# A delta-rule attention and a multiplicative FFN in one kernel: two more weight buffers, outputs without a drain, and a new order of steps

## The chip, the cores and the metric

The kernel runs on one core of a Trainium2 chip. The metric is the device time of one execution in microseconds (us). Names of the engines: PE is the TensorE matmul engine (PEld its weight loads), DVE is VectorE, ACT is ScalarE, POOL is GpSimd, and SP is SyncE, which here only issues transfers.

## The reference

The first part is a delta-rule attention over 4 batches, 8 heads, 768 tokens and a head width of 48; the second an FFN over the 3072 tokens, in which two products are multiplied before the third. The four weights arrive as float64, all other inputs as float32; the kernel computes in float32.

```python
k_n = k / (np.linalg.norm(k, axis=-1, keepdims=True) + 1e-06)
for t in range(S):
    y[:, :, t] = q[:, :, t] @ state                    # per batch and head, 48 x 48 state
    v_old = state . k_n[t]
    state = state + beta[t] * outer(k_n[t], v[t] - v_old)
x = y.transpose(0, 2, 1, 3).reshape(B * S, H * D)      # 3072 x 384
a, b = x @ w1, x @ w2                                  # 3072 x 1024 each
out = ((a * b) @ w3) @ w_out                           # 3072 x 384
```

## The kernel before

**Chunks.** The 768 tokens are cut into 12 chunks of 64. In a chunk the recurrence becomes matrix products: `scores` (steps `s0` to `s11`) multiplies keys by keys and by queries; `to_blocks` (`u`) and `inverse` (`V0` to `V5`, one for two chunks) solve the triangular systems on DVE by 31 steps of multiply and subtract in blocks of 32; `corner` (`e`) joins the blocks by products on PE; `chain` (`c`) carries the state on, by three groups of products on PE with a step of DVE behind each; `outputs` (`y`) forms the chunk's outputs, by features, in the tile `xT`. Norms are made by `squares` (`g`) and `norms` (`N`), values are scaled by `scaled_v` (`n`). `load_k`, `load_q`, `load_v`, `load_perm` (`k`, `q`, `v`, `p`) issue transfers; `by_tensor` (`K`, `Q`) transposes the first two chunks on PE, `by_vector` (`d`) the others on DVE.

**Weights.** The 36 weight pieces (`P0` to `P35`) arrive as float64 and are turned into float32 by `piece`: a transfer by SP into a `raw` buffer (line 789), two ACT instructions (797, 798), two of DVE (800, 801) and an addition on POOL (805), behind which the buffer is free. `raw` has five buffers, taken in turn, so SP holds the sixth piece until POOL has finished with the first. `P0` to `P7` are `w_out`, `P8` to `P23` are `w3`, `P24` to `P35` are `w1` and `w2`. Then `w3` is transposed (`t`) and multiplied into `w_out` (`fold`, steps `f0` to `f7`, two halves of four products each; line 849), so that the FFN has one product less. The first half of a fold needs the first four pieces of `w_out`, the second half the last four. Five raw buffers later become room for sums of weights (`T`, `W`).

**FFN.** Two chunks make a unit of 512 tokens. Steps `a`, `b`, `h`, `i`, `j` form the products with `w1` and `w2` (lines 869, 988), `S` and `G` sums of blocks on POOL, `o` the last products (1098), `x` the results and their stores.

**Order.** No scheduler orders the instructions. `ORDER` is a list of some 1,460 names written out; each name runs its generator up to the next `yield`, and every engine, and every queue, works off its instructions in the order of that text. So an instruction that waits holds all that is behind it on its engine. Pools are turned by hand: `in_turn` gives out the next buffer of a tag. The PSUM tag `w` has two pairs of banks, and one is held while an inverse keeps its matrix there; the SBUF tag `o` has two buffers (squares, results), `xT` has two (beta, the inverses' columns, then the outputs).

**Scores and outputs.** Heads go in pairs, an even one on partitions 0 to 47, an odd one on 64 to 111, and batches in two halves `z`, so that four tiles of 64 rows by 64 columns of the array can be at work together. In `scores` an even head gets one matmul of 128 columns (lines 381 to 384: keys and queries at once), an odd head two of 64 (387), with the second written to the other half of the partitions. One copy on ACT (405) takes the query part, `PT`, out of PSUM, and POOL masks it (407). Chunks 2 and 3 do that on DVE (411). In `outputs` (line 744) a chunk's 64 matmuls are of two kinds, state by query and `X` by `PT`; those that would write a bank from other rows of the array than the rest come last, behind a drain of PE:

```python
        for mode, todo in enumerate(modes):
            if mode:
                drain = pe.drain().ins
```

Eight copies of 48 x 256 on ACT (765) bring the outputs into `xT`. A float32 matmul appears as two records in the trace.

Of the kernel before, what the change touches and what calls it, by code (L numbers as in the profile page):

```python
# [39 lines left out]
V0 P0 k0 beta P18 P13 P0 P18 P0 P0 P11 g0 P13 K0 P18 K0 P11 P18 P10 P13 P13 q0 P3 P3 P11 g0 beta  # L40
beta K0 K0 K0 k1 K1 P10 P11 P12 P3 P12 g0 g0 Q0 P10 g0 g0 g0 g0 g0 P8 Q0 Q0 Q0 K1 K1 K1 Q0 K1 P3
N0 P9 k2 P8 P8 P10 s0 P8 N0 g1 s0 s0 s0 s0 s0 s0 u0 q1 P2 Q1 P9 p2 P2 P12 P12 P9 Q1 g1 Q1 Q1 P2
u0 g1 Q1 d2 d2 u0 P5 P1 t0 t0 t5 t5 P9 t2 t2 P4 P6 s1 s1 P5 P5 P2 s1 P1 s1 s1 s1 u1 g1 P1 u1 u1
t4 V0 V0 P5 V0 V0 P4 t10 P7 P4 t3 t3 V0 V0 P1 f1 P6 P6 t4 V0 P7 V0 V0 t10 t1 P14 P7 P4 V0 f0 V0
P6 P16 P16 V0 V0 P7 t1 s0 P19 P19 P19 P19 V0 f1 P17 k3 p2 v1 V0 V0 P14 P14 P14 V0 f2 P17 f2 f0 V0
f2 P15 v0 P20 f1 t11 f0 P17 P17 f5 V0 V0 P16 t11 P16 t8 P15 V1 V0 t8 f5 t9 V0 V0 t6 P15 V0 n0 n0
f5 V0 V0 V0 V0 t9 P20 P20 V0 t6 P22 P22 P22 f4 P23 P23 V0 f4 f4 P21 P21 P15 t7 t7 V0 s1 V0 V0 V0
V0 g1 d2 d2 P22 f3 f3 P24 P20 g1 g1 p3 g1 P26 p3 P30 e0 e0 e0 t12 t14 e1 e1 g1 f3 e0 e0 d3 d3 N1
s2 s2 s2 P23 P23 t12 e0 f6 e0 p4 s2 P24 e1 e1 t14 s2 e0 P24 s2 P25 c0 P26 f7 u2 P30 P24 c0 e1 e1
P21 P21 d3 d3 y0 y0 P26 P26 P31 t15 t13 s3 s3 s3 s3 s3 s3 t13 c0 n1 n1 P32 t15 u2 u2 u3 c0 P30 f7  # L50
e1 P25 P25 P31 P31 P27 c1 c1 u3 u3 f6 e1 c1 V1 V1 V1 y0 P31 f6 f7 P25 P27 V1 V1 V1 V1 P30 b1 c1
N1 b1 v2 P32 V1 V1 P27 V1 s1 y1 y1 b2 V1 d4 V1 V1 P28 P29 P32 b2 P27 V2 V1 V1 V1 y1 b3 V1 V1 P28
P28 b0 P32 c1 b2 b2 b3 b1 b1 b0 P29 P29 b0 P29 a03 a03 a02 V1 b0 V1 d4 V1 V1 a01 V1 P28 V1 V1 a02
V1 P35 a01 a00 a00 n2 n2 a04 a04 b7 P33 P33 a05 a05 P34 P34 a01 a07 b7 V1 b4 b5 V1 V1 V1 V1 k4
a01 a07 k5 b5 b3 g2 b4 V1 V1 P35 V1 V1 g2 c1 e2 e2 e2 e2 a06 a06 g2 e3 e3 e3 b3 g2 g2 a00 a02 a02
p4 v3 d4 d4 p5 a00 e2 P34 c2 c2 e2 P34 e2 b6 P35 P35 e2 c2 c2 e3 a03 g2 g2 P33 b6 y2 g2 P33 g2 d5
d5 p5 c2 c2 y2 a04 e3 s4 N2 e3 s4 a03 s4 b6 b6 s4 s4 s4 s4 T e3 T T d5 n3 d5 a04 e3 b4 b4 b7 s5
n3 k6 g3 u4 s5 s5 s5 s5 s5 s5 b5 b7 b5 a05 T c3 c3 a06 a05 a06 u5 V2 p6 g3 a07 a07 c3 c3 g3 S0 S0
S0 V2 g3 V2 V2 N2 oD0 y3 y3 V2 V2 W oA0 S0 S0 V2 V2 S0 S0 S0 c3 v5 n5 V2 V2 S0 S0 S0 S0 V2 v4 oB0
V2 V2 V2 xA0 V2 V2 xB0 V2 V2 oA0 S0 S0 S0 n4 oB0 xA0 d6 y3 k7 xA0 V2 n4 oC0 V2 V2 V2 a10 xB0 S0  # L60
V2 V2 xC0 G1 V2 xD0 a10 a10 V2 oC0 a10 a10 d6 xC0 xC0 xC0 xD0 V2 V2 i10 V2 h10 c3 c4 V2 V2 j10 V2
V2 V2 a10 h10 i10 a12 V2 V2 h10 W W a12 p6 V2 a12 a12 j12 e4 g3 g3 h10 c4 a12 h10 a12 h12 d6 d6
s5 i12 e4 e4 e4 i10 h12 h12 g3 g3 p7 g3 e4 e4 h12 N3 s4 h12 a11 a11 a11 s6 s6 i12 i12 e5 c4 j11
s6 c4 y4 y4 c4 e5 d7 d7 h11 c4 c5 a11 p7 e5 s6 a11 a11 h11 i11 i11 n5 c5 d7 d7 N3 a13 h11 h11 e5
W e5 s7 e5 a13 s7 s7 s7 s7 s7 s7 a13 a13 s6 s6 c5 i11 k8 u7 u6 g4 g4 g4 S1 V3 V3 c5 p8 h11 s6 g4
h13 a13 j13 a13 i13 h13 i13 i13 S1 h13 V3 h13 h13 V3 V3 y5 V3 V3 V3 V3 V3 V3 d8 V3 V3 V3 y5 oC1
oA1 S1 oD1 S1 S1 V3 V3 S1 xA1 c5 oA1 xA1 oB1 v6 y5 v7 a20 a20 V3 xA1 V3 V3 V3 d8 G2 V3 V3 xB1 n6
V3 V3 V3 V3 oB1 xB1 xC1 S1 j20 k9 V3 xD1 V3 V3 V3 V3 S1 oC1 a20 a20 p8 xC1 V3 xC1 h20 V3 xD1 xC1
V3 V3 V3 V3 a20 a20 i20 h20 a22 h20 g4 c5 g4 g4 g4 a22 V3 j22 d8 h20 h20 e6 i20 g4 a22 d8 a22 h22
a22 a22 i22 e6 V4 e6 c6 i20 h22 e6 i22 h22 n7 h22 e6 e6 a21 a21 a21 n6 c6 p9 c6 s8 i22 N4 h21 h22  # L70
i21 a21 s8 a21 s6 c6 y6 s8 s8 j21 s8 v8 a21 h21 i21 y6 d9 d9 e7 p9 e7 s8 s8 e7 e7 s7 h21 h21 i21
h21 a23 c6 c6 e7 a23 i23 a23 n8 n8 d9 e7 S2 N4 d9 a23 s9 s9 s9 s9 s9 n7 s9 k10 s9 u8 g5 a23 a23
c7 c7 h23 h23 i23 i23 c7 c7 g5 u9 h23 h23 V4 V4 V4 j23 h23 S2 g5 g5 V4 V4 V4 V4 p10 v9 V4 y7 y7
V4 V4 oA2 V4 V4 d10 V4 y7 V4 V4 S2 oD2 S2 d10 xA2 V4 S2 S2 oB2 oC2 V4 c7 xB2 V4 V4 V4 V4 oB2 xB2
xC2 xD2 p10 V4 V4 V4 oA2 V4 V4 a30 a30 G3 a30 a30 S2 S2 oC2 k11 V4 xC2 j30 s9 V4 xD2 xC2 V4 V4 V4
V4 V4 V4 xA2 xA2 xC2 g5 a30 h30 a30 i30 a32 h30 V4 V4 V4 e8 h30 i30 c7 a32 j32 h30 h30 g5 a32 a32
i32 g5 g5 d10 d10 i30 a32 a32 e8 h32 h32 i32 p11 e8 e8 a31 a31 c8 e8 s8 c8 g5 a31 j31 e8 c8 n9 c8
h32 h32 h32 y8 y8 c8 e9 e9 i31 d11 d11 h31 e9 e9 n9 a31 c8 s10 a31 p11 i32 N5 s10 s10 a31 h31 s10
s10 s10 s10 c9 c9 h31 e9 e9 d11 d11 u10 i31 i31 s11 a33 a33 S3 a33 v11 h31 h31 s11 s11 s11 s11
s11 a33 c9 i33 a33 a33 c9 h33 h33 s11 u11 i33 i33 j33 h33 h33 V5 V5 V5 V5 y9 S3 h33 V5 V5 V5 v10  # L80
n10 n10 oA3 S3 S3 V5 V5 oD3 V5 oB3 s10 y9 y9 oC3 V5 V5 S3 S3 V5 V5 V5 V5 V5 xA3 xB3 V5 V5 n11 V5
V5 oB3 V5 xB3 xD3 xC3 xC3 xD3 oA3 G4 a40 S3 S3 a40 a40 V5 oC3 N5 V5 V5 V5 xA3 a40 a40 xC3 h40 a40
h40 i40 V5 V5 V5 V5 h40 h40 V5 j40 h40 i40 V5 V5 V5 V5 a42 a42 a42 a42 i42 h42 a42 j42 xA3 V5 V5
a42 i40 h42 i42 h42 h42 a41 a41 a41 a41 h41 a41 V5 e10 e10 e10 e10 h42 n11 a41 i42 h41 i41 i41
i41 h41 e10 e11 h41 e10 c9 j41 a43 a43 a43 S4 c9 e11 e11 e11 h41 c10 c10 h43 c10 a43 e11 j43 xC3
a43 c10 a43 i43 h43 i43 i43 h43 h43 e11 h43 c10 c10 y10 y10 c11 s11 oD4 c11 c11 c11 oA4 xA4 y11
S4 S4 S4 oB4 oA4 y11 y11 S4 S4 S4 xA4 xB4 oB4 xB4 oC4 xC4 xA4 a50 xC4 S4 oC4 xC4 xD4 xD4 a50 G5
a50 h50 a50 a50 i50 a50 h50 i50 i50 h50 h50 j50 h50 a52 a52 a52 a52 i52 a52 a52 h52 a51 h52 i52
j52 h52 h52 h52 i51 a51 a51 a51 h51 i52 S5 a51 a51 h51 i51 j51 h51 h51 i51 a53 a53 a53 a53 h53
a53 a53 h53 j53 h51 h53 h53 h53 i53 i53 i53 xC4 o5 x5 o5 S5 S5 o5 o5 x5 S5 S5 S5 S5 o5 x5 x5 o5  # L90
x5 x5 x5 x5 x5 x5 S5 o5 x5 x5 x5 x5
# [4 lines left out]
def kernel(  # L96
# [14 lines left out]
    P = 128  # L111
# [21 lines left out]
    def half(z):  # L133
        return slice(C * z, C * z + C)
# [230 lines left out]
    def by_parity(x):  # L365
        return x.rearrange("p (a e) t -> p a e t", e=2)
# [3 lines left out]

    def scores(m):
        u = Us[m % 2][:, 0 : NR * H * C].rearrange("p (r h t) -> p r h t", r=NR, h=H)
        for r in range(NR):
            KQ = KQs[m]
            ps = two_banks()
            for h in range(H):
                for z in range(2):
                    x = KQ[feat(h % 2), NR * z + r, h // 2]
                    n = 128 * (h // 2)
                    if h % 2 == 0:  # L380
                        pe.matmul(  # L381
                            ps[half(z), 0, n : n + 128], lhsT=x[:, 0, :],
                            rhs=x.rearrange("p j t -> p (j t)"), start=True, stop=True,
                        )
                    else:
                        for j in range(2):
                            pe.matmul(  # L387
                                ps[half(z ^ j), 1, n + C * j : n + C * j + C],
                                lhsT=x[:, 0, :], rhs=x[:, j, :], start=True, stop=True,
                            )  # L390
# [13 lines left out]
            if m < 2 or m > 3:  # L404
                act.copy(out=by_parity(PT), in_=psv[:, :, :, 1, :])  # L405
                yield
                pool.tensor_tensor(  # L407
                    out=PT, in0=PT, in1=smask[:].unsqueeze(1).to_broadcast([P, H, C]), op=ALU.mult
                )
            else:  # L410
                dve.tensor_tensor(
                    out=by_parity(PT), in0=psv[:, :, :, 1, :],
                    in1=smask[:].unsqueeze(1).unsqueeze(1).to_broadcast([P, NP, 2, C]),
                    op=ALU.mult,
                )
# [295 lines left out]
    def outputs(c):  # L711
        PT, St, X, KQ = PTs[c], Ss.get(c), Xs[c], KQs[c]
        py = two_banks()
        pyv = py[:].rearrange("p x (b a t) -> p x b a t", b=B, a=2)

        def region(h, z, r):
            return pyv[feat(h // NP), (h + z) % 2, NR * z + r, h % NP // 2, :]
# [5 lines left out]
        for mode, todo in enumerate(modes):  # L723
# [8 lines left out]
            for r in range(NR if mode == 0 else 0):  # L732
# [5 lines left out]
        part = [(h // NP, (h + z) % 2) for todo in modes for h, z, *_ in todo]  # L738
        issued, n = ([], []), 0
        for mode, todo in enumerate(modes):  # L740
            if mode:
                drain = pe.drain().ins
# [7 lines left out]
        for i in issued[0]:  # L750
            in_order(i, drain)
# [7 lines left out]
        for z in range(2):  # L759
# [24 lines left out]

    def piece(n, srcs, dst):

        raw = in_turn(ffn, [P, CW, 2], "raw", 5, "raw", U32)
# [500 lines left out]
```

## Time and profile before

| What | Value |
|---|---|
| Median of 3 runs | 557.11 us (554.81 to 559.89) |
| Profiled execution, its own time | 556.14 us |
| Span of its trace | 554.1 us |
| PE busy | 520.0 us, 94% |
| DVE busy | 388.0 us, 70% |
| POOL busy | 256.6 us, 46% |
| ACT busy | 188.1 us, 34% |
| Chain that ended last | PE 74%, DVE 4%, ACT 1% of the span |
| Transferred | 52.64 MB, 95 GB/s on the mean |

The span is the time from the first to the last instruction in the trace; the execution's own time is 2.0 us more. Every duration below is from this one execution. A busy time is an engine's sum over the span, and says little on its own: a wait of DVE or ACT costs only if PE, in the end, waits for it.

### The profile page before, as it was taken

To read this page: it belongs to the slowest core of one execution; us is meant where nothing else is said; L and a number is where in the kernel's file an instruction comes from. 1 tells how busy PE (TensorE), PEld (TensorE's weight loads), DVE (VectorE), ACT (ScalarE), POOL (GpSimd) and SP (SyncE) were. 2 spreads that over 40 slices of the span, in tenths; PEclk is the share of its full clock that TensorE was granted. 3 is DMA by queue.
4 is the path that set the end of the run, shared out by engine and by line. 5 is a ranking of instruction groups with operands and counts; after the bars stand their busy time and mean duration, and the time that the engine had idled before them with its cause. 6 is when DMAs were issued, how large, how long until landed. Compare 5 with 4: busy or idle time off the path is not lost.

```text
span 554.1 us, 19883 instructions
## 1 busy us (share of the span) xinstructions
PE 520.0 (94%) x8540; PEld 446.7 (81%) x8540; DVE 388.0 (70%) x850; ACT 188.1 (34%) x393; POOL 256.6 (46%) x278
## 2 busy tenths in 40 slices
PE   2486998999999999999999999999999999999997
PEld 2473566688778988889988889988899888998897
DVE  3889999899876878659977579859587654123332
ACT  3688388954542112332022430123221121300000
POOL 8576473723659970455443355510482212342141
PEclk9998999999999999999999999999999999999999
DMA  8986987579457345455553564253411220020001
GB/s 247 197 200 211 161 224 126 138 157 151 63 80 128 76 110 82 60 100 89 99 108 64 82 120 76 92 83 46 106 31 44 63 50 2 10 66 1 0 1 57
DMA packets 197687, 52.64 MB, mean 95 GB/s; under 512 B 185344, under 2 KB 191488, under 8 KB 197600
## 3 DMA queue, kind: packets, MB, share of 16 engines
q1 hardware_dynamic: 193408, 50.59, 44.8%
q10 hardware_dynamic: 4192, 0.79, 1.0%
q8 instruction: 67, 1.10, 0.8%
q14 instruction: 20, 0.16, 0.1%
HBM read 41.25 MB, written 8.91 MB: 91 GB/s over the span
## 4 chain that ended last, share of the span: by engine, by line
PE 74%; DVE 4%; ACT 1%; issue 1%; DVEq 0%
PE ps_f L988 35%; PE ps_f L1098 19%; PE ps_w L645 5%; PE ps_w L744 4%; PE ps_f L869 4%; PE ps_w L574 2%; PE ps_w L381 1%; PE ps_w L387 1%; DVE ps_w L487 1%; DVE tb L482 1%; ACT TT L547 1%; PE ps_w L1098 1%; DVE KQ L337 0%; DVE ab L885 0%; DVE Ub L501 0%
## 5 line engine op out<-in xcount | busy, mean ns | idle before, releaser
L996 DVE TENSOR_TENSOR ab<-ab,ps_f 128x512 f32<-128x512 f32 x80 | 54.5, 682 | 58.5 <-PE ps_f L988 57.8
L1069 POOL TENSOR_TENSOR ab<-ab 128x512 f32<-128x512 f32 (+1 forms) x56 | 61.4, 1118 | 41.5 <-PE ps_f L1098 24.4
L988 PE MATMUL ps_f<-xT,w1s 128*128 128x256 f32 x320 | 78.5, 382 | 0.0
L1035 POOL TENSOR_TENSOR ab<-ab,late 128x512 f32<-128x512 f32 x19 | 24.2, 1272 | 107.6 <-DVE ab L996 106.1
L988 PEld LDWEIGHTS ps_f<-xT,w1s 128*128 128x128 f32 x320 | 59.9, 190 | 7.9
L1098 PE MATMUL ps_f<-w,ab 128*128 128x192 f32 x376 | 65.5, 328 | 0.0
L1098 PEld LDWEIGHTS ps_f<-w,ab 128*128 128x128 f32 x376 | 61.3, 190 | 1.3 <-issue 0.5
L849 PE MATMUL ps_f<-w2s,w3T 128*128 128x384 f32 x128 | 45.3, 505 | 4.9 <-POOL w2s L805 4.9
L407 POOL TENSOR_TENSOR PT<-PT,smask 128x512 f32<-128x512 f32 x20 | 25.6, 1283 | 50.9 <-ACT PT L405 50.9
L1098 PE MATMUL ps_f<-room,ab 128*128 128x192 f32 x272 | 47.2, 328 | 0.0
L498 DVE TENSOR_TENSOR ps_w<-ps_w,tb 128x31 f32<-128x31 f32 (+15 forms) x124 | 43.3, 349 | 4.2
L765 ACT COPY xT<-ps_w 48x256 f32<-48x256 f32 x96 | 30.5, 366 | 44.5 <-PE ps_w L744 44.0
L1098 PEld LDWEIGHTS ps_f<-room,ab 128*128 128x128 f32 x272 | 44.3, 190 | 0.6 <-issue 0.3
L493 DVE TENSOR_TENSOR tb<-ps_w,Ub 128x31 f32<-128x31 f32 (+15 forms) x124 | 41.9, 338 | 3.6 <-ACT ps_w L473 0.3
L1004 ACT COPY ab<-ps_f 128x512 f32<-128x512 f32 x20 | 11.7, 585 | 95.1 <-PE ps_f L988 95.0
L988 PE MATMUL ps_f<-xT,room 128*128 128x256 f32 x160 | 41.1, 384 | 0.0
L849 PEld LDWEIGHTS ps_f<-w2s,w3T 128*128 128x128 f32 x128 | 24.0, 194 | 20.4 <-POOL w2s L805 5.5
L988 PE MATMUL ps_f<-xT,w2s 128*128 128x256 f32 x160 | 40.1, 381 | 0.0
L988 PE MATMUL ps_f<-x_room,w2s 128*128 128x256 f32 x160 | 38.9, 386 | 0.0
L988 PEld LDWEIGHTS ps_f<-x_room,w2s 128*128 128x128 f32 x160 | 29.5, 190 | 5.2 <-DVE late L996 1.0
L988 PEld LDWEIGHTS ps_f<-xT,w2s 128*128 128x128 f32 x160 | 30.1, 190 | 4.1
L988 PEld LDWEIGHTS ps_f<-xT,room 128*128 128x128 f32 x160 | 29.6, 190 | 4.7 <-DVE osb L1128 0.6
(146 smaller groups left out, 1005.5 us busy)
## 6 DMA issues: line engine op xcount, KB each, us to landing
raw<-in_moe_w_dram SPq DMA_DIRECT2D x16, 512.0 KB, 5.6
vtok<-in_v_dram SPq DMA_DIRECT2D x24, 192.0 KB, 4.5
raw<-in_moe_w_dram SPq DMA_DIRECT2D x24, 192.0 KB, 4.6
out_dram<-osb SPq DMA_DIRECT2D x46, 96.0 KB, 1.7
ktok<-in_k_dram SPq DMA_DIRECT2D x44, 96.0 KB, 3.4
raw<-in_moe_w_out_dram SPq DMA_DIRECT2D x8, 384.0 KB, 4.2
perm<-in_k_dram SPq DMA_DIRECT2D x40, 64.0 KB, 3.0
perm<-in_q_dram SPq DMA_DIRECT2D x32, 64.0 KB, 2.6
```

The lines of the kernel that those rows point to most:

```text
L407: pool.tensor_tensor(out=PT, in0=PT, in1=smask[:].unsqueeze(1).to_broadcast([P, H, C]), op=ALU.mult)
L493: dve.tensor_tensor(out=tv, in0=V[:, 0 : s + 1, s : s + 1].to_broadcast([P, s + 1, n]), in1=U[:, s, s + 1 : BS].unsqueeze(1).to_broadcast( ...
L498: dve.tensor_tensor(out=o, in0=o, in1=tv, op=ALU.subtract)
L645: pe.matmul(out(ps, r, h, z), lhsT=lhs(r, h, z), rhs=rhs(r, h, z), start=True, stop=True,)
L744: i = pe.matmul(region(h, z, r), lhsT=lhs, rhs=rhs, start=part[n] not in part[:n], stop=part[n] not in part[n + 1 :],)
L765: act.copy(out=xT[f, p:NP:2, b : b + NR, cc, :].rearrange("p a r t -> p r a t"), in_=pyv[f, z, b : b + NR],)
L849: pe.matmul(ps[:, 0:DM], lhsT=w3Ts[jc, kc // 4][:, kc % 4 * P : kc % 4 * P + P], rhs=wo[:, kc], start=(kc == 0), stop=(kc == KF - 1),)
L988: pe.matmul(acc[name][:, n * i : n * i + n], lhsT=ws[b][:, P * i : P * i + P], rhs=xs[x], start=new and k == 0 and i == 0, stop=k == len(t ...
L996: dve.tensor_tensor(out=o_, in0=x, in1=acc[name], op=ALU.add)
L1035: eng.tensor_tensor(out=Z1, in0=Z1, in1=late, op=ALU.mult)
L1069: pool.tensor_tensor(out=o_, in0=x_, in1=y_, op=op)
L1098: pe.matmul(ps[b][:, b, :], lhsT=block(u, HF * f + i, z)[:, P * b : P * b + P], rhs=ws_[w][:, i], start=first and i == 0 and (b == 0 or n ...
```

## The change

There are three parts.

1. **Raw buffers.** `raw_buffer` gives the first 21 pieces seven buffers in turn. The two new ones are the halves of one `xT` buffer, which isn't otherwise in use by then. From the 22nd piece on it is five again.
2. **Nine chunks without a drain** (`SWAPPED`: 1 and 4 to 11). In their scores an odd head gets one matmul of 128 columns too, so 32 matmuls instead of 48 per chunk. `PT` is then taken out by four copies of 64 x 256 for each half of the scores, in the order that lets each head keep its own rows of the array. `outputs` gets a step ahead of its matmuls: two ACT copies bring the `z = 1` half of `X` to the other half of the partitions, into `Xc`, a buffer of the tag `o`. All 64 matmuls then go in one run, and four copies of 48 x 512 bring the outputs into `xT`. Chunk 0, which has no state part, loses its drain as well.
3. **The list.** The first nine names of `ORDER` stay, the others are put in a new order. It has the same names as often as before, but for one more of `y` for each of the nine chunks.

```diff
 ORDER = """
-V0 P0 k0 beta P18 P13 P0 P18 P0 P0 P11 g0 P13 K0 P18 K0 P11 P18 P10 P13 P13 q0 P3 P3 P11 g0 beta
+V0 P0 k0 beta P18 P13 P0 P18 P0 P18 P18 P13 P13 P11 P10 q0 P3 k1 K0 g0 g0 g0 P13 K0 K0 beta K0
...
+    SWAPPED = (1, *range(4, NCH))
...
-                    if h % 2 == 0:
+                    if h % 2 == 0 or m in SWAPPED:
                         pe.matmul(
-                            ps[half(z), 0, n : n + 128], lhsT=x[:, 0, :],
+                            ps[half(z), h % 2, n : n + 128], lhsT=x[:, 0, :],
                             rhs=x.rearrange("p j t -> p (j t)"), start=True, stop=True,
                         )
...
-                act.copy(out=by_parity(PT), in_=psv[:, :, :, 1, :])
+                if m in SWAPPED:
+                    for z in range(2):
+                        for e in range(2):
+                            act.copy(
+                                out=PT[half(e), NP * z : NP * z + NP, :],
+                                in_=psv[half(z), :, e, 1, :],
+                            )
+                else:
+                    act.copy(out=by_parity(PT), in_=psv[:, :, :, 1, :])
...
+        swapped = c in SWAPPED
+        if swapped:
+            Xc = in_turn(ffn, [P, NR * NP, D], "o", 2, "Xc")
+            for e in range(2):
+                act.copy(
+                    out=Xc[half(e)].rearrange("p (r a) d -> p r a d", r=NR),
+                    in_=X[half(1 - e)].rearrange("p r (a e) d -> p r a e d", e=2)[:, :, :, e],
+                )
+            yield
...
-        for mode, todo in enumerate(modes):
+        for mode in range(2):
+            todo = modes[0 if swapped else mode]
...
+            for r in range(NR if mode == 0 and swapped else 0):
+                for a in range(0, NP, 2):
+                    for z in range(2):
+                        for h in (a, a + 1, NP + a, NP + a + 1):
+                            x = half(h % 2)
+                            todo.append((
+                                h, z, r, Xc[x, NP * r + h // 2, :] if z else X[x, r, h, :],
+                                PT[x, r, NP * z + h // 2, :],
+                            ))
...
-            if mode:
+            if mode and todo:
                 drain = pe.drain().ins
...
+        for e in range(2):
+            f = feat(e)
+            for p in range(2 if swapped else 0):
+                act.copy(
+                    out=xT[f, p:NP:2, :, cc, :].rearrange("p a b t -> p b a t"), in_=pyv[f, p]
+                )
+        for z in range(0 if swapped else 2):
...
+    raws, more = [0], []
+
+    def raw_buffer():
+        n, k = raws[0], raws[0] % 7
+        raws[0] += 1
+        if n < 21 and k >= 5:
+            if not more:
+                t = in_turn(ffn, [P, NP, B, 2, C], "xT", 2, "more")
+                t = t[:].rearrange("p a b c t -> p (a b c t)").bitcast(U32)
+                for i in range(2):
+                    x = t[:, 2 * CW * i : 2 * CW * i + 2 * CW]
+                    more.append(x.rearrange("p (n w) -> p n w", w=2))
+            return more[k - 5]
+        return in_turn(ffn, [P, CW, 2], "raw", 5, "raw", U32)
+
     def piece(n, srcs, dst):
 
-        raw = in_turn(ffn, [P, CW, 2], "raw", 5, "raw", U32)
+        raw = raw_buffer()
```

## The prediction

> **What bounds the kernel now.** I read the page first, then the windows, the waits of PE and of SP's queue, the chain of waits, and the groups by form. Busy times of the engines, and PE in 40 slices:
>
> ```profile
> PE 520.0 (94%) x8540; PEld 446.7 (81%) x8540; DVE 388.0 (70%) x850; ACT 188.1 (34%) x393; POOL 256.6 (46%) x278
> ...
> PE   2486998999999999999999999999999999999997
> ```
>
> PE is busy 520.0 of 554.1 us, so 34.1 us is all that a better order can win. The windows say where it lies (columns: width, then PE, PEld, DVE, ACT, POOL busy, granted clock, DMA share, GB/s):
>
> ```profile
> 0.00:10.00 10.00, 2.28 (x63) 2.05 (x64) 2.62 (x4) 3.52 (x5) 8.95 (x25) 1.00 0.79 220
> 10.00:20.00 10.00, 2.64 (x28) 1.99 (x20) 8.00 (x13) 5.78 (x10) 6.39 (x6) 1.00 1.08 243
> ...
> 40.00:50.00 10.00, 5.12 (x16) 2.62 (x15) 8.96 (x21) 9.56 (x18) 6.41 (x6) 0.83 0.60 196
> 50.00:80.00 30.00, 29.86 (x109) 18.24 (x108) 28.18 (x72) 17.25 (x31) 16.02 (x17) 1.00 0.92 205
> 80.00:160.00 80.00, 75.08 (x1819) 60.40 (x1819) 73.29 (x171) 54.15 (x109) 37.28 (x40) 1.00 0.67 122
> 160.00:520.00 360.00, 358.28 (x5979) 318.65 (x5967) 239.88 (x523) 80.07 (x187) 158.03 (x168) 1.00 0.37 71
> 520.00:554.10 34.10, 30.23 (x167) 27.96 (x165) 10.18 (x18) 1.55 (x3) 9.89 (x8) 1.00 0.07 24
> ```
>
> PE idles 23.5 us before 50 us, 5.1 from 50 to 160, 1.7 in the 360 us after that, and 3.9 at the end. So there are three regimes: a head that waits for weights, a middle where DVE is busy 92% and its inverse V1 carries the chain of waits, and a long rest in which PE has no gap. In the rest a microsecond off PE's work is a microsecond off the time, and any new wait is a loss.
>
> In the head the waits are these (engine, line, waited for; us, times, longest):
>
> ```profile
> PE ps_f L350 <- DMA ktok<-in_k_dram: 15.3, 5, 5.3
> PE ps_f L849 <- POOL w2s L805: 4.9, 1, 4.9
> ...
> SPq L789 <- POOL w2s L805: 10.6, 6, 3.6
> ```
>
> The last line is the wait that two more raw buffers take away: SP holds a weight piece until POOL has freed its buffer.
>
> **Part 1, the drain in nine outputs.** One output of before in the chain of waits (start, us, what):
>
> ```profile
> 301.54 1.49 PE ps_w L744 x96
> 303.03 0.12 issue
> 303.15 0.67 PE ps_w L744 x32
> 303.81 1.92 PE ps_f L988 x8
> ```
>
> The run takes 2.27 us: 96 matmul records before the drain at 1.49/96 = 15.5 ns each, a gap of 0.12, then 32 records in 0.66, 20.7 ns each, since the array empties and fills again. In one run the 32 cost 32 x 15.5 = 0.50, so 2.27 - 1.49 - 0.50 = 0.28 us goes. Bounds: the gap alone, 0.12, and 0.43 if all 128 go at the pace of output 0 (63 records start in 0.87 us, 13.8 ns; 2.27 - 1.77 - 0.07). I take 0.28, from the same run. Nine outputs: -2.5 us (-1.1 to -3.9). Nothing hides it, as PE is the bound there.
>
> **Part 2, scores with 16 matmuls fewer per chunk.** An odd head's two matmuls of 64 columns become one of 128. The columns moved are the same. In a half of a score run (two 64-row groups by two 64-column groups) each quarter of the array moves 4 heads x 2 records x 128 columns; a record of 256 columns takes 218.8 ns (L988 x172 in 37.63 us), so 128 take 109 and the quarter 0.875 us. The half takes 0.92 from its first record to the next step (305.67 to 306.59). It is limited by columns, not by the count: I take 0. The bound is a run limited by its count: a third of 0.92 over 18 halves, -5.5 us. The Trainium skill (TensorEngine Tiling (Array Packing), Instruction Overhead) has a rule that speaks for that end: every matmul carries about 60 cycles however few columns it moves. By it the time would be that of the rival on counts below; the 0.92 against 0.875 here doesn't show it for four quarters at work together.
>
> **Part 3, what ScalarE gets.** From the groups by form (last columns: busy us, mean ns):
>
> ```profile
> L765 ACT COPY xT<-ps_w 48x256 f32<-48x256 f32 x96 | 30.5, 366 | 44.5 <-PE ps_w L744 44.0
> ...
> L405 ACT COPY PT<-ps_w 128x512 f32<-128x512 f32 x20 | 11.7, 585 | 25.5 <-DVE U L393 25.5
> ...
> L881 ACT COPY ab<-ps_f 128x256 f32<-128x256 f32 x16 | 5.7, 369 | 13.2 <-PE ps_f L869 13.1
> ...
> L1133 ACT COPY room<-ps_f 128x384 f32<-128x384 f32 x6 | 2.9, 480 | 19.2 <-PE ps_f L1098 19.2
> ```
>
> PT: one copy of 585 ns becomes four of 256 columns at 369, 1.48 us, so +0.89 in each of 18 halves, +16.0 us. Xc: two copies of 384 at 480 per chunk, +8.6 us (the far row is the strided copy L547, 1128 ns per 512, 846 here: +15.2). xT: eight of 366 become four of 585, -5.3. ACT goes from 188 to about 207 us, 37% of the span, so ACT isn't the bound. What counts is who waits:
> - A score's PSUM pair is free again only after DVE's U and the PT copies. Before, PT starts 1.02 us after the half's last record has started (306.59 to 307.61) and takes 0.58. Neighbouring copies overlap: the xT copies start 0.27 and 0.38 us apart in turn, so four take 1.29. The first half then needs 1.02 + 1.29 = 2.3 us of other PE work behind it, the second 1.02 + 2.58 - 0.92 = 2.7, as its copies queue behind the first's (before: 1.6 and 1.3). I added up the PE work by the rows between each score and the next use of its pair in the new list: chunk 7 has 1.7 and 1.7, chunk 4 2.2 and 2.2, chunk 9 2.6 and 2.8, chunk 10 2.6, all others behind 155 us 3.6 or more. Short are chunk 7 by 1.0 and chunk 4 by 0.5: +1.5 us (0 if DVE and ACT are early, 12.8 if all 18 halves showed their 0.71).
> - The y step waits for X (DVE 0.95) and now Xc (2 x 0.48), some 2.2 us. Work between in the new list: 1.4 in chunk 1, 2.6 in chunks 4, 8 and 11, 3.5 or more in the others; and the 32 state records of each run (0.5 us) come ahead of the first use of Xc. Cost 0.3 in chunk 1, in the middle where DVE leads, taken as 0; at the far row 1.5.
> - Xc takes one of two "o" buffers. In the list its last users lie a dozen steps or more back, so no store is waited for.
>
> **Part 4, the buffers and the new list in the head.** SP's order of transfers is the same for the first 387 of 498. P3 then needn't wait until 10.76, but can follow P10 at about 6.7, and k1, P12, P8, P9, k2 and q1 move up behind it. But the DMA share is 1.08 from 10 to 20 us, so the bytes don't arrive sooner there; only after 20 us (0.79, 0.88, 0.60) can they. After that ACT is the head's bound (9.2 and 9.6 of 10 us). So I counted the work ahead of V0, the first inverse, on which the middle hangs. ACT: t0, t5, t2 (3 x 0.58) and N0's three (0.6) move behind it, the PT of chunk 1 adds 0.89: -1.5 us. DVE: 32.5 us becomes 32.0, one reduction (0.54) less. The other way: K0's copy now waits for DVE behind P13, and g0's sums stand behind P10's addition on POOL, which by the rows gives ACT about as much idle time (2.2 and 2.6 us) as the waits for P3 and P12 (2.2 and 2.1) did; and the first fold waits for t4 behind u1 and V0's copies (2.2 + 1.2), some 1.7 us later than 46.03. Of these I take DVE's row, as V0 is DVE's: -0.5 (-6.3 if DVE, idle for 11.8 us before V0, lost half of that beyond its first 5.5; +3 if the late fold is never regained).
> Behind the head the lists agree more than their length shows: the PE work ahead of the corners e0, e4 and e6, of both s2, of all but four of the outputs and of the last stage is the same to 0.1 us, and DVE's work ahead of V1 (94.0), V2 and V3 is too. The steps in between only change places, so I take 0 for the rest of the list; between its links (c, e, y) the PE work in the new list is nowhere under 0.9 us, as before.
>
> **The sum.** -2.5 + 0 + 1.5 - 0.5 = -1.5 us. The profiled execution took 556.14 us (span 554.1 and 2.0 around it), so 554.6; the median of the runs, 557.11, is 1.0 above it, so I forecast 555.6 us, no change that shows: about 1%, 5.6 us, is what a measurement of this kernel can tell, with three runs from 554.81 to 559.89.
>
> **Rivals.**
> - The wider PT hand-off decides, slower. Place: the PSUM pair behind the scores of chunks 4 to 11. If a copy across 64 partitions costs what a 512-column copy does (585, not 369), starting 0.6 apart as L619's pairs do, PT takes 2.4 us, the halves need 3.4 and 4.9, and chunks 4, 7, 9 and 10 fall short by 2.7, 3.2, 2.1 and 0.8, 8.8 us in PE's rest: 555.6 - 1.5 + 8.8 = 562.9, and more where the late masks and outputs queue behind. Where the shortfalls pass the 2.5 us of the drains, at some 0.37 us from copy to copy, it decides. For: PE has no slack there, and ACT takes its work in order. Against: the 256-column rows stand at 366 and 369.
> - The head loses: fold late, and not regained before 160 us: the drains and PT, and +3: 559.1. For: ACT 9.6 of 10. Against: 5.1 us of PE's idle time between 50 and 160, which a later PE needn't take.
> - The head wins: V0 starts some 6 us sooner: 555.6 - 5.8 = 549.8. For: SP's 10.6 us of waits and DVE's idle 11.8. Against: the DMA share of 1.08 and ACT's own queue.
> - Scores are limited by counts: 555.6 - 5.5 = 550.1.
> - The drain does nothing, as the change of rows empties the array anyway: 558.1, near the forecast.
>
> **How the numbers follow.** Forecast (with the idle drain) 0.50, wide PT 0.18, late head 0.13, early head 0.13, counts 0.06. Faster by over 1% (under 551.5): 0.10 of the early head, 0.05 of the counts, 0.08 of the forecast, where the drains give their 3.9 and nothing stalls: 0.23. Slower by over 1% (over 562.7): 0.12 of the PT rival, 0.05 of the late head, 0.03 of the forecast: 0.20. Within: 0.57. The forecast's own range is 551.5 to 560; with most of the early head and of the PT rival it is 547 to 564.
>
> **What would show it.** In the profile after: L744 as one run of 128 records in 2.0 us without the gap; a score half still 0.92 us long with fewer records; PT copies near 370 ns; PE waits for PT of some 1.5 us in all behind the scores of chunks 4 and 7; SP's wait for POOL's pieces gone; the first fold at 47 to 48 us and V0 on DVE near 44. I am wrong if V0 starts before 41 or after 47, if PE idles more than 5 us between 160 and 520, or if a copy of PT takes 0.5 us or one of Xc 0.8.

## The result, and the profile after

The changed kernel took 560.64 us (median of 9 runs, 559.56 to 563.26), the kernel before 556.61 (9 runs, 554.81 to 559.89): a ratio of 1.0084, 95% interval 1.0061 to 1.0107. It is 4.0 us slower, where 1.5 us less was forecast. That is less than the 1% that the forecast said three runs can tell; with nine runs of each, the interval shows it. The profiled execution took 560.49 us, with a span of 558.4.

Busy times and PE's 40 slices, from the page after:

```profile
PE 518.7 (93%) x8252; PEld 445.0 (80%) x8252; DVE 388.8 (70%) x850; ACT 209.5 (38%) x429; POOL 255.2 (46%) x278
...
PE   2457998989999999999999999999999998999997
```

PE has 1.3 us less to do, and its last matmul comes 4.3 us later (554.5 against 550.2), so it idles more. The windows (the same columns as before) say where:

```profile
40.00:50.00 10.00, 7.12 (x49) 6.02 (x42) 8.95 (x20) 9.42 (x19) 5.93 (x7) 0.68 0.60 202
50.00:80.00 30.00, 29.81 (x112) 18.29 (x111) 28.25 (x74) 18.18 (x39) 16.37 (x16) 1.00 0.87 179
80.00:160.00 80.00, 75.00 (x1684) 59.59 (x1683) 71.81 (x158) 56.20 (x110) 38.84 (x42) 1.00 0.60 116
160.00:520.00 360.00, 355.60 (x5821) 314.77 (x5821) 242.54 (x534) 99.82 (x221) 156.43 (x166) 1.00 0.38 72
```

From 160 to 520 us PE idles 4.4 us, against 1.7 before. PE's waits in that stretch, first after, then before (two views):

```profile
PE ps_w L385 <- ACT PT L412: 1.2, 2, 0.7
PE ps_w L657 <- issue: 0.9, 1, 0.9
PE ps_w L777 <- issue: 0.8, 1, 0.8
PE ps_f L1152 <- DVE ab L1079: 0.5, 1, 0.5
PE ps_w L657 <- ACT PT L412: 0.4, 1, 0.4
PE ps_w L385 <- ACT T L611: 0.3, 1, 0.3
```

```profile
PE ps_w L744 <- issue: 0.3, 1, 0.3
PE ps_w L381 <- ACT TT L619: 0.3, 1, 0.3
```

The waits for `PT` are the ones of the forecast. "issue", time in which PE waits for nothing that the profile shows, was in nobody's sum. The chain that ended last names it too; the line of before and the one of after:

```profile
PE 74%; DVE 4%; ACT 1%; issue 1%; DVEq 0%
```

```profile
PE 72%; DVE 8%; DMA 7%; issue 4%; ACT 3%; SPq 3%; POOL 2%; DVEq 0%; POOLq 0%; ACTq 0%
```

The two lines can't be set side by side: the chain of before reaches back only to 109.6 us, the one of after to the start, and most of its 21 us of "issue" belong to other engines (6.3 us at 158.8 us to POOL). PE's own idle stretches in it are the pieces at 86.9, 93.0, 98.1, 468.7 and 473.8 us, 3.7 us together; in the chain of before there is one such piece, 0.35 us.

The delay against before, step by step: V0 starts 0.8 us late on DVE (45.1 against 44.3) and ends 1.6 late, the scores s3 (100 us) are 3.3 late, V1 3.0, V2 (174 us) 4.1, V5 3.4, the last matmul 4.3. Nearly all of it is there by 174 us; what PE loses behind that is about as much as the drains give back there.

### The profile page after: what moved, and what is told of

Read it like the earlier page. It is cut to its first block, busy times and chain, and to the rows that moved or that the text cites. A ratio compares the mean times of both kernels' runs of the same rounds, so it can differ in the third digit from the quotient of the medians.

```text
span 558.4 us, 19356 instructions
## 1 busy us (share of the span) xinstructions
PE 518.7 (93%) x8252; PEld 445.0 (80%) x8252; DVE 388.8 (70%) x850; ACT 209.5 (38%) x429; POOL 255.2 (46%) x278
## 3 DMA queue, kind: packets, MB, share of 16 engines
q8 instruction: 65, 1.06, 0.8%
## 4 chain that ended last, share of the span: by engine, by line
PE 72%; DVE 8%; DMA 7%; issue 4%; ACT 3%; SPq 3%; POOL 2%; DVEq 0%; POOLq 0%; ACTq 0%
PE ps_f L1042 33%; PE ps_f L1152 19%; PE ps_w L657 5%; PE ps_w L777 3%; PE ps_f L923 3%; PE ps_w L385 3%; SPq L251 2%; PE ps_w L586 2%; DVE tb L494 2%; DVE ps_w L499 2%; DMA X<-in_q_dram 2%; PE ps_f L903 1%; DMA raw<-in_moe_w_dram 1%; POOL w2s L859 1%; DMA Ub<-Ud 1%
## 5 line engine op out<-in xcount | busy, mean ns | idle before, releaser
L903 PE MATMUL ps_f<-w2s,w3T 128*128 128x384 f32 x128 | 44.0, 494 | 0.0
L283 POOL TENSOR_TENSOR sq<-ktok 128x384 f32<-128x384 f32 x24 | 20.1, 845 | 37.8 <-DMA out_dram<-osb 19.5
L385 PE MATMUL ps_w<-KQ 48*64 48x128 f32 x672 | 30.3, 295 | 7.6 <-ACT KQ L360 5.4
L385 PEld LDWEIGHTS ps_w<-KQ 48*64 48x64 f32 x672 | 24.8, 146 | 11.7 <-ACT KQ L360 6.3
L412 ACT COPY PT<-ps_w 64x256 f32<-64x256 f32 x72 | 26.3, 366 | 19.9 <-DVE U L397 19.1
```

The source lines that it names most:

```text
L385: pe.matmul(ps[half(z), h % 2, n : n + 128], lhsT=x[:, 0, :], rhs=x.rearrange("p j t -> p (j t)"), start=True, stop=True,)
L412: act.copy(out=PT[half(e), NP * z : NP * z + NP, :], in_=psv[half(z), :, e, 1, :],)
L903: pe.matmul(ps[:, 0:DM], lhsT=w3Ts[jc, kc // 4][:, kc % 4 * P : kc % 4 * P + P], rhs=wo[:, kc], start=(kc == 0), stop=(kc == KF - 1),)
```

## The experiments

Ratios are to runs of the kernel before on the same chip, whose medians were 556.0 to 557.8 us; medians from different chips can differ by up to 1.8 us for that alone. Twenty kernels are compared in all; the table behind the experiments puts them side by side.

**Which part costs.** The first four runs take the parts apart, by three theories: T, the new list makes the head late; U, ScalarE's extra copies; W, transfers crowd one another.

Buffers alone, under the old list and with the drains:

```diff
 kernel before
-        raw = in_turn(ffn, [P, CW, 2], "raw", 5, "raw", U32)
+        raw = raw_buffer()
```

> The old list and outputs with a drain, but seven raw buffers for the first 21 pieces. Theory T: the buffers only let transfers start earlier, in a stretch where the DMA share is 1.08 anyway: 0 to -2 us, 555 to 557. Theory W (pieces that start earlier crowd the keys and queries, whose landing PE waits for: 8.1 us for X in the changed kernel against 1.6): the head is later, +2 to +4 us, 559 to 561.

557.07 us, 1.0010 (0.9984 to 1.0037): nothing. (Here, as in e1, e6 and e9, chunk 0 runs without its drain, as in the changed kernel.)

Nine chunks without a drain alone, under the old list (one more `y` behind the chain's last product of the chunk) and with five buffers:

```diff
 kernel before
+    SWAPPED = (1, *range(4, NCH))
-... c4 ...
+... c4 y4 ...
```

> The old list with the nine outputs without a drain (the step that makes Xc stands right behind the chain's X), five raw buffers. Theory T (the new list's head is late: the first fold starts at 48.7 instead of 46.0 us and V0 at 45.1 instead of 44.3, and the middle passes this on): the head is the old one, so nine drains give -3.0 us (0.33 each) and the wider PT hand-off takes back 1.0 at chunk 7, 0.6 at 9 and 0.6 at 10; about 556, within 1 us of before. Theory U (ScalarE's extra copies delay DVE and PE wherever they stand): +3 to +4, 560.

570.31 us, 1.0258 (1.0227 to 1.0288): much slower, though PE's matmuls in it are those of the changed kernel, 8252 records.

The changed kernel with five buffers:

```diff
 changed kernel
-        raw = raw_buffer()
+        raw = in_turn(ffn, [P, CW, 2], "raw", 5, "raw", U32)
```

> The changed kernel with five raw buffers throughout. Theory T: the order of steps is what is late, and the buffers only help it: the time of the changed kernel, 560.6, or 1 to 3 us more. Theory W: without the crowding 2 to 4 us less, 557 to 558.

578.64 us, 1.0401 (1.0365 to 1.0436). The new list needs the two buffers: without them V0 starts 4.9 us late and ends 13.5 late. Crowding (W) is out, since more buffers are better or nothing.

The old list's head (its first 254 names, up to e0) in the changed kernel:

```diff
 changed kernel
-ORDER: new list
+ORDER: old list up to the first e0, then the other names in the new list's order
```

> The changed kernel, with the names of the old list up to its first e0 (254 names) and then all others in the new list's order. Theory T: V0 starts at 44.3 again, V1 near 106, and 3 to 4 us go: 556.5 to 557.5. Theory U: the middle loses its 2 to 3 us by ScalarE's copies whatever the head: 559.5 to 560.

567.98 us, 1.0219 (1.0186 to 1.0252): slower, though V0 is only 0.3 us late, so a late head made by the new list (T) doesn't explain the 4 us. No figure of T, U or W for these four runs was above 564 us: none of the three foresaw 570, 579 or 568.

The next four ask whether ScalarE's copies cost (A), or whether list, yields and buffers fit only one another (M).

```diff
 e6: changed kernel           e7: changed kernel
+    SWAPPED = ()             +    SWAPPED = tuple(range(4, NCH))
 (the nine added y dropped)   (chunk 1's added y dropped)
```

> The changed kernel with the new list and seven buffers, but no chunk treated the new way (SWAPPED empty, and the nine added names of y left out). The theory of the late head has fallen with the old-head run (568.0) and the five-buffer run (578.6). Theory A (ScalarE's copies of the nine chunks are the cost; under the old list they cost 14 us net of the drains, and the new list exists to take 10 of them back): without them 553 to 557, not above before. Rival M (lists, yields and buffers fit only one another, and any mismatch costs, whatever ScalarE does): 562 to 570.

565.77 us, 1.0143 (1.0105 to 1.0182).

> The changed kernel with chunk 1 as it was before (SWAPPED is 4 to 11). Theory A: chunk 1's copies stand where ScalarE is 8 to 10 tenths busy (V1 started 3.0 us late in the changed kernel, and 5.8 with the old list), so 3 to 4 us go: 556.5 to 558. Rival M: 560 to 565.

563.76 us, 1.0113 (1.0083 to 1.0143).

In the kernel before, only the copy of `PT` in those nine chunks is cut:

```diff
 kernel before
-                act.copy(out=by_parity(PT), in_=psv[:, :, :, 1, :])
+                if m == 1 or m > 3:
+                    for z in range(2):
+                        for a in range(0, NP, 2):
+                            act.copy(out=by_parity(PT)[half(z), a : a + 2], in_=psv[half(z), a : a + 2, :, 1, :])
+                else: ...
```

> The kernel before, with its list, buffers, matmuls and drains; only the one PT copy of each score half of the nine chunks is cut into four of 64 x 256 (ScalarE's added cost of PT alone, no Xc, no y step added). Theory A: most of the 14 us of the old-list run plus nothing from the drains: +8 to +15, 565 to 571. Rival M: 556 to 558, as nothing in the order has changed.

560.39 us, 1.0050 (1.0024 to 1.0076): about 2.6 us.

```diff
 kernel before
+    SWAPPED = (1,)
-... c1 ...
+... c1 y1 ...
```

> The old list and five buffers with the new way for chunk 1 alone. Theory A: 5 of the 14 us of the old-list run are lost here (V1 5.8 us late in that run), less 0.4 of one drain: 561 to 562. Rival M (a share by the number of chunks): 14/9 us, 557.5 to 558.5.

567.89 us, 1.0177 (1.0145 to 1.0209). One chunk's outputs would hardly cost 10 us by a wait of their own, and the loss was spread: 1.9 us between c0 and s3, 2.6 more by V1, 4.7 more by V2. ScalarE's copies (A) fall as the whole cause. M had e6 and e7 right (562 to 570, 560 to 565) and missed e8 (556 to 558) and e9 (557.5 to 558.5); as a mere saying, "any mismatch costs" contradicts none of the eight, and it says nothing of how.

**What "issue" is.** One of these stretches in the timeline of the changed kernel's PE (start, us, what, idle before):

```profile
86.65 0.25 PE L586 MATMUL ps_w<-TT,late 64*33 64x32 f32 x4
88.07 0.22 PE L586 MATMUL ps_w<-tb,late 64*33 64x32 f32 x2 [1.18 <-issue]
```

PE stops in the middle of one corner, 64 matmuls long, and the profile shows nothing that it waits for. The page has a queue that brings no data:

```profile
q8 instruction: 65, 1.06, 0.8%
```

65 packets of 16 KB: 8252 weight loads and 8252 matmuls at 64 bytes make 1.06 MB, so this is PE's own program, 256 instructions to a block. I set the packets of that queue against PE's records. Each longer stop in the changed kernel, from its matmuls' start times:

```
PE stands        line   block's transfer    resumes after its end
 86.70..88.07    L586    85.70..86.58       1.50
 92.80..93.57    L657    90.89..92.23       1.33
 97.90..98.37    L777    95.74..96.99       1.39
386.36..386.67   L657   384.25..385.17      1.50
468.53..469.69   L657   467.31..468.27      1.42
473.54..474.52   L777   472.21..473.15      1.36
```

PE's records (weight loads, matmuls, its semaphore waits) numbered from the start of the trace, and the blocks of that queue from 0, every one of these stops lies ahead of the same place: record 256 x k + 449, counted from 0, with block k the one that has just landed. So it is over all 20 traces: of the pauses over 0.3 us inside runs of small matmuls behind 80 us, 100 stand at this one of 256 places, and no other place has more than six. I count as a stop a pause of 0.13 us or more at this place that ends 1.1 to 1.8 us behind the end of its block's transfer: 134 in the 20 traces, the median 1.4 us behind it. A block's transfer starts once PE has passed about record 256 x k + 146; from there to its use 303 records are in hand. From passing that record to the block's use took 4 to 5 us at the median in the stretches of these traces behind 80 us, over 6.5 us in one case in ten. Two records of an FFN product, a weight load and a matmul, take 0.22 us (17 such matmuls in 3.71 us at 249.8 us), so there 303 records last some 33 us, by estimate. But the dense runs eat them: a corner 128 records in 0.57 us, a chain step 128 in 0.93, an output 256 in 1.94. Where such runs follow one another, PE is through the stock in 3 to 5 us, and whether a block's edge falls there decides whether PE stops. Behind 40 us these stops sum to 0.6 us before and 5.0 us after, 4.4 us more; the loss is 4.0 (medians) or 4.3 (last matmul). (One more, of 0.5 us at 30 us in the changed kernel, isn't counted: PE waits 4.9 us for ScalarE right behind it.) Of the 5.0, 2.6 lie between 86 and 99 us, where the delay arises, and 2.4 behind 386 us, where the drains pay for them.

The Trainium skill (Runtime: NRT & Kernel Launch, Instruction fetch mechanics) describes blocks of 16 KiB, 256 instructions, as the packets here are, and calls the cost of crossing a boundary mostly hidden. Here it isn't: single stops reach 2.3 us, and their sum 10 us in the worst kernel.

**Shifting the program.** Theory B (late blocks) can be tried without touching order, buffers, copies or waits: some matmuls ahead of everything move all that follows against the block edges. A model of it takes PE's records of one trace without their stops, a fixed time from record 146 to use, and adds up what is missing at record 449. By it the kernel before stands nearly best: of the 128 even shifts only one gives less with 4.6 us from trigger to use (4.9 us of stops; mean over the shifts 9.7, worst 14.4). Its absolute figures are off, 4.9 us against 0.6 measured before and 2.5 against 5.0 after, so only its differences are used. The matmuls go behind the twelve beta transposes at 12 us, or ahead of the first fold:

```diff
+        for n in range(75):
+            x = half(n % 2)
+            pe.matmul(ps[feat(n % 2), 0, NR * H : NR * H + 4], lhsT=ident[x, 0:D], rhs=ident[x, 0:4], start=True, stop=True)
```

One thing is wrong in the first eight of these expectations: such a float32 matmul stands as two weight loads and two matmuls, four records instead of two. The true shifts are 300 (p1, q1; 44 beyond a whole block), 512 (p2; two whole blocks), 24 (p3), 220 (p4), 308 (q2; 52), 136 (q3) and 336 (q4; 80). The model for these shifts, with 4.6 us, against the unshifted kernel: p1 and q1 +4.6 us, p2 0, p3 -0.4, p4 +2.6, q2 -3.6, q3 +0.5, q4 +4.9.

> The kernel before, with 75 tiny matmuls (64x48 tile, 4 columns, into columns that nobody reads) behind the twelve beta transposes at 12 us, where TensorE idles until 17 us. They move every later TensorE instruction by 150 places in the 16 KB blocks (256 instructions) in which TensorE's program is fetched. Theory B (blocks): wherever the profile after shows TensorE idle for 'issue', TensorE stands at the 450th instruction counted from a block's number times 256 and resumes 1.3 to 1.6 us after that block's transfer ended; a dense run of small matmuls eats the stock before the next block lands, and where the dense runs lie in the blocks sets the time. From the trace of before, with 4.0 us from the instruction that triggers a block to its use, a shift of 150 is the worst: 8.5 us of such stalls against 1.1 unshifted (with 4.6 us, 14.4 against 4.9). B expects 563 to 567 us, stalls at the 450th instruction all along. Theory M (order, yields and buffers fit only one another): nothing of these moves, 556 to 558 us.

> The same with 128 tiny matmuls: 256 instructions, one whole block, so that the later instructions stand at the same places in their blocks as in the kernel before. It costs the pads' own time (1 to 2 us, in an idle stretch) and nothing else. Theory B: 556 to 558 us, the same as before, though it has more added than the run with 75. Theory M: 556 to 558 too. If the pads themselves or the TensorE clock that they wake early cost or bring something, this run shows it alone.

p1 562.63 us, 1.0100 (1.0069 to 1.0132); p2 561.88, 1.0090 (1.0063 to 1.0118). Both are slower, in different places. The 128 matmuls of p2 last until 23.1 us, so that V0 starts 4.9 us late; behind V0 it loses 0.9. The 75 of p1 make V0 1.0 late, and behind it 6.4 us go. Stops: 6.2 us in p1, 0.9 in p2. PE's waits from 80 to 520 us in p2 have no row with "issue" at all.

> The kernel before with 75 tiny matmuls (64x48 tile, 4 columns, into columns of a fold's bank that nobody reads) ahead of the first fold at 46 us, so that the head is left alone. Every later TensorE instruction stands 150 places further in its block of 256. Theory B (blocks of TensorE's program that land late): from before's trace 8.5 us of stalls with 4.0 us from a block's trigger to its use, against 1.1 unshifted; p1 had 6.2 us of them in its profile; the run takes 561 to 564 us, with the first product of vectors (V0) where it was. Theory M (the order fits only its own buffers and yields, blocks don't matter): 556 to 558 us.

The same without touching the head: 560.84 us, 1.0083 (1.0053 to 1.0113), just under B's 561 to 564, with V0 0.4 us earlier than before. Rows of its waits from 80 to 520 us:

```profile
PE ps_w L645 <- issue: 2.4, 3, 0.9
PE ps_w L574 <- ACT late L599: 1.0, 1, 1.0
PE ps_f L861 <- issue: 0.9, 1, 0.9
...
PE ps_w L574 <- issue: 0.4, 1, 0.4
PE ps_w L381 <- issue: 0.3, 1, 0.3
PE ps_f L840 <- issue: 0.2, 1, 0.2
```

The kernel before, with its order, buffers and copies as they were, loses 4.8 us by a shift alone, about as much as the whole change costs. Theory M said 556 to 558.

> The kernel before with nine chunks' outputs the new way under the old order and five raw buffers (570.3 us, 10.2 us of stalls), and 77 tiny matmuls ahead of the first fold: a shift of 154, the best for it (2.5 us of stalls by the model with 4.0 us from trigger to use, against 7.1 unshifted; 6.4 against 12.2 with 4.6 us). Theory B: 5 to 6 us less, 564 to 566 us. Theory M: 570 to 571 us.

564.17 us, 1.0148 (1.0106 to 1.0191): 6.1 us less than the 570.31 without the shift, stops 6.2 us against 10.2. What is left are waits for ScalarE (`PT` 3.6 us from 80 to 520 us). The profile is of one of the slower executions, 567.90 us.

> The kernel before with chunk 1's outputs alone the new way (567.9 us, 10.2 us of stalls), and 34 tiny matmuls ahead of the first fold: a shift of 68 (1.2 us by the model against 4.5 with 4.0 us, 5.8 against 10.0 with 4.6). Theory B: 3 to 6 us less, 562 to 565 us. Theory M: 568 us.

568.32 us, 1.0214 (1.0170 to 1.0258), stops 10.2 us as without the shift: the gain didn't come. By the true shift none was due.

> The changed kernel with 6 tiny matmuls in the same place: a shift of 12 instructions, where the trace of the changed kernel gives the fewest stalls (0.0 with 4.0 us from trigger to use, 1.0 with 4.6; unshifted 1.2 and 2.5, measured 5.0 in six stalls). Theory B: 3 to 5 us less than the changed kernel, 556 to 558 us, that is the kernel before or a little under. Theory M: 560 to 561 us, as without the pads.

566.41 us (560.66 to 570.06), 1.0145 (1.0102 to 1.0187). By the true shift of 24 little was due, but 5.8 us more than the changed kernel (3.4 by the ratios) isn't explained: the profile is of the fastest execution, 560.66 us, with 6.7 us of stops, and the slower ones left no trace.

> The changed kernel with 55 tiny matmuls: a shift of 110 instructions, the worst for it (8.9 us of stalls with 4.0 us from trigger to use, 13.8 with 4.6). Theory B: 566 to 570 us. Theory M: 560 to 561 us.

565.16 us, 1.0135 (1.0101 to 1.0169), stops 6.3 us. The direction is right; the size by the true shift is 2.6, against 4.5 by the medians and 2.8 by the ratios.

> The changed kernel with 84 tiny matmuls ahead of the first fold and 44 more ahead of an a product at 151 us: shifts of 168 until there and of a whole block, 256, from there on. With 4.6 us from trigger to use the model gives 0.7 us of stalls against 2.5 unshifted, with 5.2 us 4.8 against 8.1 (measured 5.0 in the changed kernel). Theory B: 2 to 4 us less than the changed kernel, 556.5 to 558.5 us, about the kernel before. Theory M: 560 to 561.5 us.

567.17 us, 1.0192 (1.0159 to 1.0225), a failed design: the 84 matmuls ran from 48.4 to 55.3 us, in the way of the folds (ScalarE's first copy of a fold is 10.0 us later than in the kernel before), and the 44 never ran, since the product they were tied to doesn't come up so often. Its stops, 4.8 us, are not the 4.9 us more that the model has for its true shift. With the head so changed, it tells little of the question.

The last two shift the changed kernel with that put right.

> The changed kernel with 27 tiny matmuls (a shift of 108) at 12 us alone. By the model with 4.6 us from trigger to use: 1.4 us of stalls until 149 us against 1.8 unshifted, 9.8 against 0.4 from 149 to 400 us, 2.2 against 0.3 after that. Theory B: 7 to 11 us more than the changed kernel, 567 to 571 us, lost between 150 and 400 us, each time at the 450th instruction of a block's number times 256. Theory M: 560 to 561 us.

567.88 us, 1.0203 (1.0179 to 1.0227): 7.2 us more than the changed kernel, with 10.4 us of stops, 6.2 of them between 180 and 400 us. Two of them in the timeline:

```profile
231.01 0.79 PE L657 MATMUL ps_w<-X,ktok 64*64 64x48 f32 x41
233.34 0.55 PE L657 MATMUL ps_w<-X,ktok 64*64 64x48 f32 x23 [1.55 <-issue]
```

```profile
311.46 0.62 PE L777 MATMUL ps_w<-KQ,S 48*48 48x64 f32 x30
313.50 0.27 PE L777 MATMUL ps_w<-KQ,S 48*48 48x64 f32 x2 [1.42 <-issue]
```

A chain step of 64 matmuls and an output of 128 break in two. B had given 7 to 11 us more, between 150 and 400 us: that is the size and, for most of the stops, the place. But 2.8 us of stops lie ahead of 125 us, and V0 is 1.6 us later than in the changed kernel. M gave 560 to 561.

> The changed kernel with 42 tiny matmuls (two pairs each, four instructions: a shift of 168) behind the twelve beta transposes at 12 us, where TensorE idles until 18 us, and 20 more (a shift of 248 in all) ahead of an a product at 151 us, where they cost about 0.9 us of TensorE's time. Theory B: of the 2.6 us of stalls that the changed kernel had at 85 to 100 us at most 1 is left (by the model with 5.2 us from trigger to use 0.6 against 4.0), the rest of the kernel as before at 2 to 3 us of stalls; with the pads' 0.9 the run takes 558.5 to 560 us, and the lead of 2 us is seen at the second product of vectors (V1) at 106 us. Theory M: 561 to 562 us, with V1 where the changed kernel has it.

560.63 us, 1.0076 (1.0052 to 1.0100), where B had given 558.5 to 560: no gain in all. The stops at 86, 93 and 98 us are gone but for 0.2 us, and s3 is only 1.4 us late instead of 3.3; then one block is 1.9 us late in a chain step at 101.5 us and takes it back, so that V1 starts 0.2 us earlier than in the changed kernel, where B had 2. Stops 3.9 us, and the 20 matmuls at 151 us cost their 0.9.

| Kernel | Median, us | Stops, us | Lost from V0 to the last matmul, us |
|---|---|---|---|
| before | 556.61 | 0.6 | 0 |
| changed | 560.64 | 5.0 | 3.5 |
| e2, buffers alone | 557.07 | 0.1 | 1.5 |
| e8, four copies alone | 560.39 | 1.7 | 2.5 |
| p2, whole blocks | 561.88 | 0.9 | 0.9 |
| r1, changed, two shifts | 560.63 | 3.9 | 3.0 |
| q1, before, shift 44 | 560.84 | 5.7 | 4.2 |
| p1, before, shift 44 | 562.63 | 6.2 | 6.4 |
| e7, without chunk 1 | 563.76 | 6.2 | 5.9 |
| e6, new list and seven | 565.77 | 5.8 | 6.3 |
| p3, changed, shift 24 | 566.41 | 6.7 | 4.1 |
| p4, changed, shift 220 | 565.16 | 6.3 | 7.2 |
| r2, changed, shift 108 | 567.88 | 10.4 | 9.9 |
| e9, chunk 1 alone | 567.89 | 10.2 | 12.3 |
| q3, e9, shift 136 | 568.32 | 10.2 | 14.7 |
| e1, outputs alone | 570.31 | 10.2 | 13.9 |
| q2, e1, shift 52 | 564.17 | 6.2 | 11.8 |

(The medians are over all runs, stops and losses of the one profiled execution, which in e7, q2 and q3 was 2.3 to 3.7 us slower than the median and in p3 5.8 us faster. e4, e5 and q4, with 19.2, 12.5 and 10.4 us lost and 6.1, 6.9 and 4.8 us of stops, lose 13.9, 7.6 and 7.8 us of it by V1, mostly by waits for weight pieces, for folds and between DVE and PE.) Stops are the larger part of most losses; where they are not, as in q2, waits for ScalarE and for weights are part of the rest. Another part is the clock. In e1, e9, q2 and q3 the granted clock was half in two stretches of 3.4 to 6.8 us behind 55 us, in e7, p4 and r2 in one of 3.4, each begun during a stop or wait of PE or within 1.2 us of its end; the kernel before and the changed one have none from 55 to 545 us. In r2's, at 302 us behind a stop of 1.3 us, eight FFN matmuls took 3.60 us, against 1.99 at 311 us in the changed kernel. So a long stop can cost more than its length.

What is shown: a shift alone moves the kernel before by 4.8 us and the changed one by 7.2, with 5.1 and 5.4 us more of stops. What is only argued: that the changed kernel would be at or under the kernel before without its 5.0 us of stops; no shift tried gave them back. A straight line through the losses of the changed kernel and its shifts r1, p3, p4 and r2 meets no stops at -1.4 us, which is an estimate from five executions that scatter. Also open is why some blocks take 3 us and others 8 from trigger to use. The load of the DMA engines doesn't tell them apart: a block's transfer starts 1.6 us after its trigger at the median where their busy share is under 0.1, and 2.1 us where it is over 0.9.

No version here beats the kernel before.

## Why the prediction was right or wrong

**The forecast itself.** -1.5 us was forecast, +4.0 came: wrong in its sign. 560.64 us lies just outside the forecast's own range, 551.5 to 560, and inside the wide one, 547 to 564, and the change stayed within 1%, which had been given 0.57.

**Part 1, drains: right.** An output runs in 1.94 us instead of 2.27, 0.33 less against 0.28, from the chain of waits after:

```profile
253.52 1.94 PE ps_w L777 x128
255.46 1.66 PE ps_f L1152 x9
```

The rival "the drain does nothing" falls. Undrained, an output also takes its 256 records out of the stock of instructions in 1.94 us.

**Part 2, scores: right.** A half still takes 0.92 us to a step that follows in small tiles (302.71 - 301.79), with 32 matmul records instead of 48: the rival on counts falls.

```profile
301.79 1.10 PE L385 MATMUL ps_w<-KQ 48*64 48x128 f32 x32
302.71 0.63 PE L777 MATMUL ps_w<-KQ,S 48*48 48x64 f32 x32
```

**Part 3, ScalarE: right.** Groups by form after:

```profile
L412 ACT COPY PT<-ps_w 64x256 f32<-64x256 f32 x72 | 26.3, 366 | 19.9 <-DVE U L397 19.1
...
L795 ACT COPY xT<-ps_w 48x512 f32<-48x512 f32 x36 | 19.1, 579 | 30.0 <-PE ps_w L777 29.8
...
L729 ACT COPY Xc<-X 64x384 f32<-64x384 f32 x18 | 9.2, 510 | 21.8 <-DVE X L697 10.0 <-issue 6.4 <-POOL ab L1089 3.1
```

366 ns for 369, 579 for 585, 510 for 480; ACT is busy 209.5 us for 207. PE's waits for `PT` behind 160 us come to 1.2 + 0.4 = 1.6 us, against 1.5, and stand where they were expected: 0.7 us behind the scores of chunk 4, 0.5 and 0.4 at the second half of those of chunk 7 and right behind it. The wide rival, at 585 ns, falls.

**Part 4: the step that failed.** In the head -0.5 was taken and +0.8 came (V0 at 45.1). The row that it was taken from came true: DVE has 0.7 us less to do ahead of V0. But it stands idle longer, 14.7 us instead of 13.1. PE waited 5.4 us for the second chunk's `KQ` copies and ran that chunk's scores at half clock behind it, so DVE's first `U` of them starts at 39.7 us instead of 38.9, and V0 is late by the same 0.8. The first fold ran at 48.7, later than the 47 to 48 given. From PE's waits after:

```profile
PE ps_f L350 <- DMA X<-in_q_dram: 8.1, 2, 6.5
PE ps_f L350 <- DMA ktok<-in_k_dram: 7.8, 2, 5.0
PE ps_w L385 <- ACT KQ L360: 5.4, 2, 4.9
```

SP's wait for POOL's pieces, foreseen as gone, is still there: the rows for line 843 on POOL's `w`, `w2s` and `w1s` sum to 16.6 us, those for 789 to 17.7 before.

The larger error is "I take 0 for the rest of the list". The argument weighed the PE work between links, where only order and waits count. It had no term for PE's program: 288 records of either kind fewer, and steps in other places, move every dense run against the block edges. That term measured 5.0 - 0.6 = 4.4 us. The terms that were sized hold up: from V0 to the last matmul 3.5 us were lost, and without the 4.4 it would be -0.9, if each stop costs its length, where drains and `PT` had given -2.5 + 1.5 = -1.0. That they agree to 0.1 is in part luck, as the drains measured 9 x 0.33 = 3.0. That the stops are there and how long they are is measured; that the change would have won without them is not.

**The rivals.** "The head loses" came nearest in time, 559.1, but not by its mechanism, a fold that is never regained: most of the loss has no wait for the fold in it.

**What was to show it.** PE idle over 5 us from 160 to 520 us, one of the signs of being wrong, was nearly met (4.4): 1.6 of it by the waits for `PT` that the text had named, 1.7 by "issue", which it hadn't.

## What to carry to other kernels

In a kernel where one engine runs without gaps, read the "issue" rows of its waits and the packets of its instruction queue before pricing a change at nothing: dense runs of tiny instructions can outrun the loading of the program. An order can happen to suit its block edges, as by the model the one before does, so an edit that adds or removes instructions ahead of dense runs can cost some microseconds that no count of work shows. To tell such a cost from a real one, run the edit at two or three shifts (a few idle matmuls at the start), and count how many instructions each of them really makes.

## What the runs showed of the hardware

- PE's program comes in blocks of 16 KB, whose transfer takes 0.9 to 1.4 us in eight cases of ten and is of use some 1.4 us after its end. PE can go no further than record 256 x k + 448 until block k is there, and with dense runs of small matmuls it gets there first. For none of the 1306 blocks of the 20 traces did it pass that record sooner than 1.2 us after the block's transfer.
- With the same program up to s1, e6 and e7 differ by 1.3 us at V0 (47.1 and 48.4 us). The difference is there at 24 us, in ScalarE's copies behind the first keys, and doesn't grow, although the granted clock of e7 was half from 36.9 to 47.1 us and that of e6 was not. That it comes from when the transfers landed is not shown.
- After PE's wait of 4.9 us at 31 to 36 us in the changed kernel, the granted clock was half from 32.8 to 43.0 us, and the second chunk's scores took from 35.9 to 41.4 us, against 36.6 to 39.0 before.
